# A fused RWKV5 and tanh-shrink kernel: u spread by TensorE, tile 0's first product by units, the last output in two parts, and a new written order

## The chip, the core and the metric

The kernel runs on one NeuronCore of a Trainium2 chip. The metric is device time in microseconds (us). Engines are named as the profile names them: PE is TensorE (PEld its weight loads), DVE is VectorE, ACT is ScalarE, POOL is GpSimd, SP is SyncE, which here only issues transfers; SPq and ACTq are the transfer-issuing instructions of SP and ACT.

## The reference, cut to what matters

```python
# attention: B, H, S, D = 4, 8, 768, 48; r, k, v float32; w, u are (H, D)
for t in range(S):
    cur = einsum('bhd,bhe->bhde', u[None] * k[:, :, t], v[:, :, t])
    y[:, :, t] = einsum('bhd,bhde->bhe', r[:, :, t], state + cur)
    state = w[None, :, :, None] * state + einsum('bhd,bhe->bhde', k[:, :, t], v[:, :, t])
x = y.transpose(0, 2, 1, 3).reshape(3072, 384)
# dense: w_in is (384, 2048), w_out is (2048, 384), both float64
h = x @ w_in
g = h - tanh(h)
out = g @ w_out          # (3072, 384) float32
```

## The kernel before, in words

**Units.** The sequence is cut into chunks of 64 steps. A unit `n` is one chunk of two of the four batches, 128 rows in all (function `unit`, with `ch, half = divmod(n, 2)`); there are 24. A unit loads r, k and v (`fetch`, L644, six transfers of 64 rows of 8 heads by 48 numbers), turns r and k by TensorE (`turn`, L656) into `x_ps`, scales them by powers of the decay into `rT` (DVE, L660) and `kT` (DVE L665, or an ACT copy, L692), forms the products of k and r within the chunk (`levels`, into `x_ps`, L606), masks them into `at` (DVE, L830) over a diagonal that ACT has written (`at`, L704) from `du`, the sum of r, k and u over a head (`rk`, L696; `rk` by `ub`, L824; `du`, L700), multiplies by v (`outputs`, into `yk_ps`), copies the result out (ACT: `xt` and `rest`, L765), and adds to the state (`state`, DVE, L792), which the next unit of the same two batches reads (`from_state`). Since `yk_ps` is one tile, a unit's `from_state` also waits until the unit before it has been copied out and added to its state. `ub` is u on all 128 partitions: before, one transfer at L568 writes it, reading u's 1536 bytes once for every partition. Units 0 and 1 differ: they have no state, and unit 0 takes its diagonal as a product with u (`own_k`, `own_levels`).

**Tiles of the dense part.** Two units make a token tile `j` of 256 rows. For each pair `f` of 128 columns of d_ff the function `hidden` makes h (`Dense.h`, L217, two halves of three products 128x256), g = h - tanh(h) in several ACT and DVE steps with a series for small h (L224 to L246), and the product with w_out (`Dense.o`, L254; later by a seven-product scheme, L307). The first tile of all is tile 0, f = 0 ("m == 0"); its h needs the `xt` of units 0 and 1 and the first piece of w_in.

**Weights.** w_in and w_out come as 64-bit floats in 16 pieces of 768 KB. A piece of w_in is two transfers on SP and two on POOL (`st`, L171); seven instructions turn it into float32: DVE L185, L186, ACT L187, L188, DVE L189, L190, L191 (`convert`).

**What sets the order.** All work is entered as tasks in a `Plan`; a table `ORDER`, two characters for each task, says in which order they are written (`written`). Each engine runs its own instructions in that order and waits where a tile is not ready. A number past the last task stands for a fill: a product of the identity that nobody reads, 512 or 256 columns wide (`fills`, L534), put where PE would have nothing to do. Transfers issued by SP and ACT take eight landing flags in turn (DMAHW0 to DMAHW7 in the listings below), so each waits until the one eight places before it has landed. 12 of the 24 units come before the seven-product part, one after another.

**The end.** The last tile (j = 11, f = 14) is done alone: `o` of the first 128 rows, then `o` of the second, each two products 128x384; DVE adds the sums of the rest (`empty`, L267 for the first half, L265 for the second) into `last`; after a branch that is not taken, four transfers (L1247) write `last` out, two on SP and two on ACT, 64 rows each.

Of the kernel before, what the change touches and what calls it, by code (L numbers as in the profile page):

```python
# [10 lines left out]
F32 = mybir.dt.float32  # L11
# [23 lines left out]
OWN = 1  # L35
SWAP = 2
# [9 lines left out]
    "00010J2i2j2k2f2g2h0H2m2l2nbWbW020K030I040605bWbX2q3435362o3231330A2s0F0B0C2r2ubWbX2x072v2y082w2t0T092z0L380M3U3C"  # L46
    "2+2p0N37393A3G2_3V3W0O3E0U3H3S3I3B3J3D3R3T3F0P3KbWbWbX3L0V3u3b300S3MbX3c3v3w0Q3N3a3f3s3O3g3P3r3t3e0R3Y3Q3hbX8D0w"
    "3d3i0W3k3X3Z3_3j0X4P430Y8E0d3l4O4Q0Z444L40458F4M4N3m0a463y0D0b3+3n0E0c423o41bY8P150e473x3z3p4p0f8H484Z4o4q0g4V4a"
    "0h494l8I4bbY4A4R0i4c4m4n4W3q4B4U0j4S4T8Q4v0l4C4X5I4Y4J4D4d8L4K5GbZ4e4I0k5J5K8R4F8G5F5H4f4H8J4G8KbZ4u8S134g4z8U8M"
    "8T4+4w4s4h0m8N4_4x4i8O4E5i4y4j5j5k500n525P4r4t8V4k5f8d8W515T0t0o5U8e536C0p5V5g5h8p8X5W5M0q6D6E5X540r8h5O0s555L5N"  # L50
    "5Q6A8q8Y56696B5R8Z5S5t5A6c578f5E5u5m8g5B5Y8i5v5lba5n595p8j5C8a585D6Z8b5Z8t0u6a6b8k8s5o5w8l6d6e5a8m8c6F5q5b6J8n14"
    "6N6G6H5r5c6O738o5s775d5x8w74755y6P8r8u915z6Q5e76786n8v6K6f8x5+6R6g6h6o6p6I5_926L7T8y7U7V609D7X6M67617W7Y6q6j656S"
    "7H636r0v687A668z6T956494936i98966U7IJx9762JyJz6k7J6V9EJ+6l6W8+J_K06m6X797B9G996s1D9H7h129F6Y9I9A9R907D7K6tKP9S9K"
    "7L7a9L6u9T7i9U7j0G7C0x9J7E6vKL9d7FKMKN0y8_7Z7b7d9e6w9MKOKQ9V726x9B7G6_1L9Y7k6z707M0zK16+719f9C7N9W9h9Z7c9X7e9iKs"
    "9a7O7lKu16K9K2K39N7PKAKvKw6y9O7g7fKrKt7QKZKa9r0+7RKR179g0_7m9Q9P9j9k9b187n10197o119s7p9l1T1U1E9c1F7q1A1G7vA19m7t"
    "9v1B7u1H7xA21C7w9u7y9t9n9yA41e1fKB1V9w1W1I1gKC1h9oLF1JA5LGLHAF9x1M9p1NA3AGA81O9z9qAR9+KDA6ASA7A9AJKb9_AIAAAUAMA0"
    "1PKc1QABAH1RAKAfAL1SATAg1iAVANAWAYAXAC1jADAZ1kArK6AEAaLIAhAsKWAi1xAOAkLJLKAjAPLl1lAmLmLnAnAQAuAvAtAyB3Aw1mAlB4Az"
    "AxLo1KLpLqAbB51XB6AoBFA+B71YB8BABG1Z1n1aBT1oBIBJBBAc2G2HBHL31p2FB9L4BUAdBMBKBCBf1bBWAeL5BVAp1cBYBXBNBgBLBaBbAqBi"
    "LTBh1dA_7S23241q2526B01rMABO1sKSKTB1BtBk1yBj1z1tBuB2Bm1+1uBD1_1vBZBE1wBlBvBcBPBy20KxBxBQBwKyKzBnBz2PB_2EC327B+28"
    "C4Bo29BRCH2A21C7BSCIC52BC6C0BdCK22CJCACLBe2XC82CM9MBCMCTCOC92ICN2DBp2J2QBq2RBr2SCUCPMf2TLzMgMhCBChCWCCCVBsCYCiCQ"  # L60
    "CXKdCbC1N3L+CZN4N52UC2CkCj2VCmCDCl2W2KCaCE2LCoCnCt2M2NCuCcD5CFCxCpCwCvCqD6CyCGC+CRD82OD7CzDK2Y2Z2aDL2bCSD92cDADC"
    "CdDBDDC_DZCfDM2dDNCe2eDaCgDECrD0DcDODFCsDbDRDGDdDPDgDoDQ85De86DpDfDS7rD1DrDhDq87EEDTD3DsDUDiEFDtDVDvD2EHDH81DuDW"
    "89ETEIDjEGELEJEUD4DkEK88EiDwEW8AEVDxDIEXEYDJDXEaDy7sDlEjEMENExEk8BElLUEmEy8CEZLVEnEbDYEoEqEzDmEpEOEcEPFNErE_DzE+"
    "FOF0EQF1D+F3DnFQ82FPD_F2EdFSE1EeFTE2FcF4EfFRE3E4E0FdE5EsE6EtE7ERE8FeEBFfE9FUFhESEuFVFgEDFrECFWF5FjEgF6FsEhFtFvEv"
    "FwFXFuFzFYFiEw7zFxEAG4FyF7FZFkG5Fl83F8FmG684G9FnG8F9F+G7FAGWGB7+FBGXFCFDFEFaFFGYGaFGFKGbGlGCGAFLGZF_FbGdFoGmGeGD"
# [1214 lines left out]
```

## Time and profile before

| what | us |
|---|---|
| median of 3 runs | 579.41 (578.5 to 583.4) |
| the profiled execution, whole | 582.91 |
| its span, from the first to the last instruction | 581.2 |
| PE busy in the span | 563.5 |
| DVE busy | 432.1 |
| ACT busy | 404.1 |

The profile has a page (busy time of each engine; the span in 40 slices; the chain that ended last), and answers by view: the timeline gives each instruction's start and length, with the idle time of its engine before it and what ended that; the view of waits adds these up; the view of windows gives each engine's busy time in a stretch, with the granted PE clock and the share of the core's 16 DMA engines (which can come out above 1). PE's busy time includes the fills, and a PE row `x6` is three products, since a float32 product is recorded in two passes.

### The profile page before, as it was taken

The page shows a single profiled execution, that of the slowest core. Times are in us where ns is not written, and L with a number is a line of the kernel's source. Part 1 is how long each engine was busy: PE and PEld are TensorE (multiplying, and loading weights), DVE is VectorE, ACT ScalarE, POOL GpSimd, SP SyncE. Part 2 cuts the span into 40 slices and gives each one's busy share as a digit, 9 for nine tenths or more (in the row PEclk, how much of TensorE's full clock was granted, in tenths as well). Part 3 has the DMA queues.
Part 4 walks back from the last instruction along what each step waited for, and adds up shares of the span by engine and source line. Part 5 has one row for each costly group of instructions (what it writes and reads, how often), then busy time and mean ns, then how long its engine had stood idle before and what let it go on. Part 6 is the DMA issues. An engine that isn't in the chain of part 4 may idle for free.

```text
span 581.2 us, 14164 instructions
## 1 busy us (share of the span) xinstructions
PE 563.5 (97%) x5487; PEld 481.5 (83%) x5487; DVE 432.1 (74%) x720; ACT 404.1 (70%) x926; POOL 202.5 (35%) x366
## 2 busy tenths in 40 slices
PE   7879999999999999999999999999999999999996
PEld 4557777777677789999899899999899898999994
DVE  5789977988999888776888897387685774565435
ACT  2689999998868666455784875766785668666560
POOL 5102211300000146353446355282454263554430
PEclk9899999999999999999999999999999999999998
DMA  8988657446640000032244352442123010010001
GB/s 130 162 204 137 125 100 189 103 76 167 114 120 15 1 1 12 17 55 41 40 74 86 62 94 39 72 86 39 25 50 60 16 34 7 3 29 2 14 16 32
DMA packets 138548, 38.48 MB, mean 66 GB/s; under 512 B 130760, under 2 KB 132904, under 8 KB 138472
## 3 DMA queue, kind: packets, MB, share of 16 engines
q1 hardware_dynamic: 130140, 29.71, 28.1%
q0 software_dynamic: 4992, 6.99, 5.3%
q10 hardware_dynamic: 3340, 0.79, 0.9%
q8 instruction: 45, 0.74, 0.5%
q14 instruction: 31, 0.25, 0.1%
HBM read 31.66 MB, written 4.72 MB: 63 GB/s over the span
## 4 chain that ended last, share of the span: by engine, by line
PE 79%; DMA 1%; ACT 1%; POOL 0%; DVE 0%; issue 0%; DVEq 0%; POOLq 0%
PE h L217 39%; PE p L307 28%; PE o L254 7%; PE yk_ps L606 5%; DMA xt<-rest 1%; PE p L254 0%; ACT xt L765 0%; POOL xt L786 0%; ACT rest L765 0%; ACT kT L692 0%; DVE rk L696 0%; DVE state L792 0%; DVE last L265 0%; PE x_ps L606 0%; DVEq L696 0%
## 5 line engine op out<-in xcount | busy, mean ns | idle before, releaser
L217 PE MATMUL h<-xt,w_in_sb 128*128 128x256 f32 x1152 | 269.0, 381 | 0.4 <-DMA xt<-rest 0.2
L217 PEld LDWEIGHTS h<-xt,w_in_sb 128*128 128x128 f32 x1152 | 214.8, 190 | 33.1 <-DVE w_in_sb L191 0.9
L290 POOL TENSOR_TENSOR sg<-g 128x256 f32<-128x256 f32 x69 | 55.9, 811 | 200.8 <-DVE g L246 147.0
L242 DVE TENSOR_TENSOR g<-h,th 128x512 f32<-128x512 f32 x96 | 65.8, 686 | 61.8 <-ACT tg L233 20.7
L229 ACT ACTIVATE s<-h 128x512 f32<-128x512 f32 x96 | 57.1, 595 | 54.5 <-PE h L217 40.0
L244 DVE TENSOR_TENSOR tg<-s,tg 128x512 f32<-128x512 f32 x96 | 71.7, 751 | 31.2 <-ACT s L224 27.7
L307 PE MATMUL p<-mixed,sg 128*128 128x192 f32 x426 | 93.0, 327 | 0.0
L246 DVE COPY_PREDICATED g<-small,tg 128x512 f32<-128x512 int32 x96 | 74.3, 783 | 12.6 <-ACT small L235 9.9
L231 ACT ACTIVATE th<-h 128x512 f32<-128x512 f32 x96 | 56.8, 593 | 35.0 <-PE h L217 34.7
L307 PEld LDWEIGHTS p<-mixed,sg 128*128 128x128 f32 x426 | 73.5, 190 | 1.4
L233 ACT ACTIVATE tg<-h 128x512 f32<-128x512 f32 x96 | 56.6, 592 | 22.9 <-DVE g L246 13.3
L307 PE MATMUL p<-w_out_sb,g 128*128 128x192 f32 x284 | 69.9, 328 | 0.0
L235 ACT ACTIVATE small<-s,smallb 128x512 f32<-128x512 f32 x96 | 68.5, 720 | 1.2
L254 PE MATMUL o<-w_out_sb,g 128*128 128x384 f32 x192 | 67.2, 489 | 0.1
L224 ACT ACTIVATE s<-s 128x512 f32<-128x512 f32 x96 | 60.1, 630 | 1.1
L786 POOL DMA_DIRECT2D xt<-rest x66 | 32.6, 498 | 68.9 <-ACT rest L765 68.4
L307 PEld LDWEIGHTS p<-w_out_sb,g 128*128 128x128 f32 x284 | 51.1, 190 | 2.7
L254 PEld LDWEIGHTS o<-w_out_sb,g 128*128 128x128 f32 x192 | 35.9, 190 | 19.4 <-issue 0.2
L704 ACT ACTIVATE at<-same,du 128x64 f32<-128x64 f32 x184 | 47.7, 340 | 5.0 <-DVE du L700 4.8
L292 POOL TENSOR_TENSOR sg<-sg,g 128x128 f32<-128x128 f32 x69 | 39.9, 581 | 3.6
L294 POOL TENSOR_TENSOR sg<-sg,g 128x128 f32<-128x128 f32 x69 | 38.1, 559 | 3.0
L307 PE MATMUL p<-w_out_sb,sg 128*128 128x192 f32 x142 | 34.9, 328 | 0.0
(127 smaller groups left out, 653.0 us busy)
## 6 DMA issues: line engine op xcount, KB each, us to landing
st<-in_moe_w_out_dram SPq DMA_DIRECT2D x8, 768.0 KB, 5.5
st<-in_moe_w_in_dram SPq DMA_DIRECT2D x16, 288.0 KB, 5.0
rt<-in_r_dram SPq DMA_DIRECT2D x46, 96.0 KB, 3.4
vt<-in_v_dram SPq DMA_DIRECT2D x46, 96.0 KB, 3.0
kt<-in_k_dram SPq DMA_DIRECT2D x44, 96.0 KB, 3.1
out_dram<-o POOLq DMA_DIRECT2D x44, 96.0 KB, 2.1
st<-in_moe_w_in_dram POOLq DMA_DIRECT2D x16, 96.0 KB, 5.8
parts<-in_k_dram SPq DMA_DIRECT2D x48, 32.0 KB, 2.1
```

Of the source, the lines that this page charges most:

```text
L217: self.nc.tensor.matmul(t.h2[:, z], self.w_in_sb[:, t.f // 2, kk, z * 128 : (z + 1) * 128], self.xts[t.j][:, kk].rearrange("p b t -> p (b ...
L224: A.activation(t.s, t.s, AF.Square, scale=G3)
L229: A.activation(out, t.h, AF.Arctan, scale=G2)
L231: A.activation(out, t.h, AF.Tanh)
L233: A.activation(out, t.h, AF.Tanh, scale=G1)
L235: A.activation(out, t.s, AF.Relu, bias=self.smallb, scale=-1.0)
L242: V.tensor_tensor(t.g, t.h, t.th, ALU.subtract)
L244: V.tensor_tensor(t.tg, t.s, t.tg, ALU.mult)
L246: V.copy_predicated(t.g, t.small.bitcast(I32), t.tg)
L254: self.nc.tensor.matmul(self.outs[i], t.g2[:, z, i * C : (i + 1) * C], self.w_out_sb[:, t.f + z, :], start=t.first and z == 0, stop=t.last ...
L290: add(t.s4[:, :2], g[:, 0::3], g[:, 1:2].to_broadcast([128, 2, C]), ALU.add)
L307: self.nc.tensor.matmul(ps[bank][:, half * n : (half + 1) * n], a, b, start=t.first and half == 0, stop=t.last, skip_group_check=True)
```

## The change

Four things are done together.

1. **u on all partitions by TensorE.** The transfer at L568 goes. u's rows already lie in the tile `rows` (with w's), loaded by the first transfers. Four small products of 8 rows by 96 columns, whose left side is a column of the identity repeated 128 times, put each row on all partitions, into a bank that unit 1 uses later; ACT copies it into `ub`.
2. **Tile 0's first h by units.** Its h, six products of 256 columns, becomes twelve of 128 columns: first the two halves for unit 0's rows, then the two for unit 1's. The fills that may stand there are entered anew.
3. **The last output in two parts.** `o` of the last 128 rows is made for columns 0 to 255 and then 256 to 383, and DVE adds each part as it is done. The last two transfers, 64 whole rows on each of SP and ACT before, become columns 0 to 255 of 128 rows on ACT and the other 128 columns on SP.
4. **A new table ORDER.** 15 fills (8 wide, 7 narrow) become 13 (8 wide, 5 narrow).

```diff
+LAST = 256
...
 ORDER = (
-    "00010J2i2j2k2f2g2h0H2m2l2nbWbW020K030I040605bWbX2q3435362o3231330A2s0F0B0C2r2ubWbX2x072v2y082w2t0T092z0L380M3U3C"
+    "00012j2k2l2g2h2i2m2n2o0I0Kbbbc020F030J040L2r36353706052p320G072s33342tbc080A0B0C2v2y092z0w2u382u393A0U2x0W2qbb2+0M"
...
-    def h(self, t, z):
+    def h(self, t, z, slot=None):
         d = self.d
+        if slot is not None:
+            if not hasattr(t, "h2"):
+                t.h2 = self.ps_d.tile([128, 2, d.NT], F32, name="h", tag="h")
+                t.h = t.h2.rearrange("p z t -> p (z t)")
+            for kk in range(d.NK):
+                self.nc.tensor.matmul(t.h2[:, z, slot * C : (slot + 1) * C], self.w_in_sb[:, t.f // 2, kk, z * 128 : (z + 1) * 128],
+                                      self.xts[t.j][:, kk, slot], start=kk == 0, stop=kk == d.NK - 1, skip_group_check=True)
+            return
...
-    def o(self, t, half):
+    def o(self, t, half, n=None):
...
-            self.nc.tensor.matmul(self.outs[i], t.g2[:, z, i * C : (i + 1) * C], self.w_out_sb[:, t.f + z, :],
-                                  start=t.first and z == 0, stop=t.last and z == 1)
+            cols = slice(0, self.d.DM) if n is None else n
+            self.nc.tensor.matmul(self.outs[i][:, cols], t.g2[:, z, i * C : (i + 1) * C], self.w_out_sb[:, t.f + z, cols],
+                                  start=t.first and z == 0, stop=t.last and z == 1, skip_group_check=n is not None)
...
+        if n is not None:
+            part = self.sums[at] if n.start == 0 else self.sums.pop(at)
+            a, b, op = (part, self.outs[i], ALU.subtract) if t.j in self.negative else (self.outs[i], part, ALU.add)
+            t.o = self.last[:, i]
+            self.nc.vector.tensor_tensor(t.o[:, n], a[:, n], b[:, n], op)
+            return
...
+    ub_ps = x_banks[1][:, 0, : H * D].rearrange("s (h d) -> s h d", h=H)
+
+    def spread_u():
+
+        for p in range(NP):
+            put_u = ident[: 2 * NP, NP + p : NP + p + 1].to_broadcast([2 * NP, 128])
+            T.matmul(ub_ps[:, 2 * p : 2 * p + 2], put_u, rows[:, :, :D], start=True, stop=True)
...
-        bonus = add("SP", .65, lambda: Q.dma_start(
-            out=ub.rearrange("p h d -> p (h d)"),
-            in_=bass.AP(tensor=u.tensor, offset=u.offset, ap=[[0, 128], [1, H * D]])), data=.7)
+        plan.at = "ub"
+        now = add("PE", .5, spread_u, landed, steps=16)
+        plan.at = None
+        bonus = add("ACT", .5, lambda: A.copy(ub, ub_ps), [now])
...
+            if m == 0:
+                now = add("PE", .66, lambda: dense.h(t, 0, 0), filled[j, "all"][:1] + [converted[piece]], due, steps=12)
+                plan.fills.append(([], now, fills(idle)))
+                now = add("PE", .66, lambda: dense.h(t, 1, 0), [now], due, steps=12)
+                now = add("PE", .66, lambda: dense.h(t, 0, 1), filled[j, "all"] + [now], due, steps=12)
+                plan.fills.append(([flagged], now, fills(tab)))
+                x.h = add("PE", .66, lambda: dense.h(t, 1, 1), [now], due + 1.3, steps=12)
...
+            whole = fs[1] == d.NF
+            if whole and j == d.NB - 1:
+                x.empty.append(add("DVE", .47, lambda: dense.empty(t, 0), [now], due + 3 * pace))
+                for n, cost, of in ((slice(0, LAST), .87, .38), (slice(LAST, d.DM), .43, .26)):
+                    now = add("PE", cost, lambda n=n: dense.o(t, 1, n), [now] + b1.emptied, due + 2 * pace + 1.3, steps=8)
+                    x.empty.append(add("DVE", of, lambda n=n: dense.empty(t, 1, n), [now, x.empty[-1]], due + 3 * pace))
+                x.o = now
+                return
...
-    for b in range(d.B):
-        queue = (nc.sync, nc.scalar)[b % 2]
-        queue.dma_start(out=out[(b + 1) * d.S - SHORT : (b + 1) * d.S, :],
-                        in_=shared["last"][b % 2 * SHORT : (b % 2 + 1) * SHORT, b // 2, :])
+    rows = out.rearrange("(b s) n -> b s n", b=d.B)[:, d.S - SHORT :]
+    for b in range(2):
+        (nc.sync, nc.scalar)[b].dma_start(out=rows[b], in_=last[b * SHORT : (b + 1) * SHORT, 0])
+    for queue, cols in ((nc.scalar, slice(0, LAST)), (nc.sync, slice(LAST, d.DM))):
+        queue.dma_start(out=rows[2:, :, cols], in_=last[:, 1, cols])
```

What the table does is seen in the instructions as each engine gets them. Numbers such as `first_k_123` or `rt_107` name the buffer: 122, 106, 116 are unit 0's k, r and v, 123, 107, 117 unit 1's, 108 and 118 unit 2's. Names of lines are those of each kernel; the changed one has them some 16 to 26 lines further down.

**Place 1: SP, the first transfers**, with what each waits for (a landing flag is named DMAHW). Before:

```order
L171 DMA st<-in_moe_w_in_dram 48x3x256 [waits DMAHW0_49]
L644 DMA vt_116<-in_v_dram 64x8x48 [waits DMAHW2_49]
L644 DMA first_k_123<-in_k_dram 64x8x48 [waits DMAHW4_49]
L644 DMA rt_107<-in_r_dram 64x8x48 [waits DMAHW5_49]
L568 DMA ub<-in_u_dram 128x384 [waits DMAHW6_49]
L644 DMA kt<-in_k_dram 64x8x48 [waits DMAHW7_49]
L644 DMA vt_117<-in_v_dram 64x8x48 [waits DMAHW0_49]
```

Now:

```order
L670 DMA vt_116<-in_v_dram 64x8x48
L172 DMA st<-in_moe_w_in_dram 48x3x256 [waits DMAHW0_49]
L172 DMA st<-in_moe_w_in_dram 48x3x256 [waits DMAHW1_49]
L670 DMA first_k_123<-in_k_dram 64x8x48 [waits DMAHW3_49]
L670 DMA rt_107<-in_r_dram 64x8x48 [waits DMAHW4_49]
L670 DMA vt_117<-in_v_dram 64x8x48 [waits DMAHW5_49]
L670 DMA kt<-in_k_dram 64x8x48 [waits DMAHW6_49]
```

ub is gone; the SP part of w_in's first piece, of which one transfer stood ahead of unit 0's k before, now follows unit 0's v; and unit 1's r waits for the landing of a transfer that was issued earlier.

**Place 2: ACT and DVE between unit 2's output and unit 3's start.** On ACT `at_133` is unit 3's diagonal, `xt`, `rest` are unit 2's output, `kT` is unit 3's, and `tg`, `s` belong to tile 0. Before:

```order
L229 ACT_TABLE_LOAD
L229 ACTIVATE s<-h 128x512
L704 ACTIVATE at_133<-same,du 128x64 x4
L765 COPY xt<-yk_ps 64x3x64 x4
L692 COPY kT<-x_ps_146 128x512
L765 COPY rest<-yk_ps 64x64 x4
L704 ACTIVATE at_133<-same,du 128x64 x4
L233 ACTIVATE tg<-h 128x512
```

Now:

```order
L242 ACTIVATE tg<-h 128x512
L730 ACTIVATE at_133<-same,du 128x64 x4
L791 COPY xt<-yk_ps 64x3x64 x4
L791 COPY rest<-yk_ps 64x64 x4
L718 COPY kT<-x_ps_146 128x512
L238 ACT_TABLE_LOAD
L238 ACTIVATE s<-h 128x512
L730 ACTIVATE at_133<-same,du 128x64 x4
```

The table load and `s` have moved from before unit 2's copies to behind them and behind unit 3's `kT`; `tg` has moved ahead. On DVE, at the same place and with what each waits for, before:

```order
L567 TENSOR_SCALAR flag<-h 1x1 [waits PE_49]
L191 TENSOR_TENSOR w_in_sb<-w_in_sb,power 128x768 [waits DVE_49]
L660 TENSOR_TENSOR rT<-x_ps_146,power 128x512 [waits Activation_49]
L185 TENSOR_SCALAR power<-st 128x768 [waits DMAHW6_49]
L792 TENSOR_TENSOR state_126<-yk_ps,state_126 128x8x48 [waits Activation_49]
L186 TENSOR_SCALAR w_out_sb<-st 128x768
```

Now:

```order
L686 TENSOR_TENSOR rT<-x_ps_146,power 128x512 [waits PE_49]
L192 TENSOR_TENSOR w_in_sb<-w_in_sb,power 128x768 [waits DVE_49]
L186 TENSOR_SCALAR power<-st 128x768 [waits DMAHW5_49]
L818 TENSOR_TENSOR state_126<-yk_ps,state_126 128x8x48 [waits Activation_49]
L187 TENSOR_SCALAR w_out_sb<-st 128x768
```

Unit 3's `rT` has moved ahead of the last step of w_in's second piece, and it waits for PE alone; before, it stood behind ACT's `kT`, which reads the same bank, and waited for ACT.

**Place 3: PE over the same stretch.** `at_132`, `vt_118` are unit 2's, `rt_106` unit 3's r; `state_127` is read by unit 3; L534 and L558 are fills. Before:

```order
L217 MATMUL h<-xt,w_in_sb 128x256 x3
L656 MATMUL x_ps_146<-ident,kw_113 128x128 x4
L606 MATMUL yk_ps<-at_132,vt_118 64x64 x16
L606 MATMUL yk_ps<-vt_118,kw_112 64x48 x16
L566 MATMUL h<-one,ok 1x1
L656 MATMUL x_ps_146<-ident,rt_106 128x128 x4
L534 MATMUL x_ps_150<-ident 128x512
L217 MATMUL h<-xt,w_in_sb 128x256 x3
L606 MATMUL yk_ps<-rT,state_127 64x64 x16
```

Now:

```order
L591 MATMUL h<-one,ok 1x1
L219 MATMUL h<-xt,w_in_sb 128x128 x6
L682 MATMUL x_ps_146<-ident,kw_113 128x128 x4
L632 MATMUL yk_ps<-at_132,vt_118 64x64 x16
L632 MATMUL yk_ps<-vt_118,kw_112 64x48 x16
L682 MATMUL x_ps_146<-ident,rt_106 128x128 x4
L558 MATMUL x_ps_150<-ident 128x512 x3
L632 MATMUL yk_ps<-rT,state_127 64x64 x16
```

The second half of tile 0's h has become the two parts for unit 1's rows, and tile 1's first h, which stood ahead of unit 3's start, now follows it; three wide fills stand there instead of one.

More of the change, by code (lines that the diff above doesn't have):

```diff
@@ L51 @@
[L51 to L65, printed above, removed]
@@ L548, in lay_out @@
                for e, at, x in (("SP", 0, w), ("ACT", NP, u))]
+        landed = now
         cols = add("PE", .25, lambda: T.transpose(cols_ps, rows.rearrange("p i d -> p (i d)"), ident[: 2 * NP, : 2 * NP]), now)
@@ L805, in unit @@
                 in_k = add("SP", 4.8, lambda: spread_out(k, 1), [b2.kT, *freed], data=.8)
-            x.turn = None if turned else add("PE", .46, lambda: turn(rt, r_ps), [x.r] + free, steps=8)
+            x.turn = None if turned else add("PE", .46, lambda: turn(rt, r_ps), [x.r] + free + [bonus] * (n == 1), steps=8)
             x.kw = add(*own_at, lambda: V_or_G.tensor_tensor(kw[:, :, :D], t.kt[:, :, :D], w_down, ALU.mult), [x.k, downs, b2.out])
@@ L920, in hidden @@
                 return
-            whole = fs[1] == d.NF
             for i in range(L):
```

81 lines of the change are left out of this document (48 added, 33 removed).

## The prediction

> **What bounds the kernel now.** I read the page's busy times and slices first, then the view of windows, then PE's waits.
>
> ```profile
> PE 563.5 (97%) x5487; PEld 481.5 (83%) x5487; DVE 432.1 (74%) x720; ACT 404.1 (70%) x926; POOL 202.5 (35%) x366
> ...
> PE   7879999999999999999999999999999999999996
> ```
>
> PE is busy for 97% of 581.2 us, and its digits are 9 from the fifth slice on: over the whole, TensorE bounds. The change takes no work from PE, so it can gain only where PE is not full: the first four slices (58 us) and the last. Windows show the first part:
>
> ```profile
> core 0: us, PE busy (x) PEld busy (x) DVE busy (x) ACT busy (x) POOL busy (x), PEclk, DMA share, GB/s
> 20.00:30.00 10.00, 7.72 (x139) 5.59 (x135) 6.94 (x13) 6.43 (x22) 1.78 (x4) 0.83 1.06 140
> 30.00:40.00 10.00, 8.22 (x184) 6.27 (x185) 7.92 (x15) 8.01 (x23) 0.00 (x0) 1.00 0.82 192
> 40.00:50.00 10.00, 8.59 (x219) 6.32 (x218) 9.51 (x16) 9.25 (x27) 3.43 (x7) 1.00 0.79 182
> 50.00:100.00 50.00, 49.12 (x932) 37.94 (x930) 42.47 (x76) 48.60 (x146) 9.17 (x19) 1.00 0.72 141
> ```
>
> PE loses 2.28, 1.78 and 1.41 us between 20 and 50, and some of its busy time there is fills; from 50 on it loses 0.88 us in 50. So the question is when PE gets to its first `o` of tile 0, from which on it is full:
>
> ```profile
> 50.21 2.75 PE L254 MATMUL o<-w_out_sb,g 128*128 128x384 f32 x8
> ```
>
> Whatever comes earlier at 50.21 comes off the end, as long as ACT, busy 48.60 of the 50 us behind it, keeps up. Before 50 PE is not the bound; what it waits for comes from DVE, and up to 30 us DVE waits for transfers.
>
> **Part A, the transfers (items 1 and 4, place 1).** DVE's waits that name a transfer, in its own in-order queue:
>
> ```profile
> 17.07 0.56 DVE L824 TENSOR_TENSOR rk<-rk,ub 128x384 f32<-128x384 f32 x1 [1.11 <-DMA ub<-in_u_dram]
> ...
> 27.56 0.56 DVE L185 TENSOR_SCALAR power<-st 128x768 uint32<-128x768 uint32 x1 [1.03 <-DMA st<-in_moe_w_in_dram]
> ...
> 29.82 0.56 DVE L696 TENSOR_TENSOR rk<-rt,kt 128x384 f32<-128x384 f32 x1 [0.76 <-DMA rt<-in_r_dram]
> ```
>
> 1.11 + 1.03 + 0.76 = 2.9 us. The first is u's copy itself, which goes. The other two are late because of a hole in the transfers:
>
> ```profile
> 8.00:12.00 4.00, 3.46 (x76) 2.35 (x75) 1.64 (x4) 2.08 (x7) 1.21 (x6) 1.00 1.21 165
> 12.00:16.00 4.00, 3.11 (x93) 2.58 (x92) 3.73 (x7) 2.20 (x4) 0.97 (x2) 1.00 0.56 123
> 16.00:22.00 6.00, 3.95 (x42) 2.12 (x42) 4.09 (x7) 3.32 (x13) 1.27 (x3) 0.96 1.16 191
> 22.00:30.00 8.00, 6.61 (x133) 4.89 (x131) 5.74 (x11) 5.25 (x16) 0.51 (x1) 0.82 1.04 125
> ...
> SPq L644 <- DMA vt<-in_v_dram: 2.6, 1, 2.6
> ...
> 10.81 0.59 SPq L644 DMA_DIRECT2D rt<-in_r_dram  x1
> ```
>
> The share (seventh value) is 1.21 and 1.16 on either side and 0.56 between: 4 x (1 - 0.56/1.18) = 2.1 us in which the queues ran dry, because SP stood 2.6 us at unit 1's r (until 10.81) for unit 0's v to land. Now that row waits for an earlier transfer, and SP can send unit 1's data and two of unit 2's without a stop. Without ub (128 times 1536 bytes, 196 KB, at 165 to 191 GB/s) another 1.0 to 1.2 us are free. Together 3.1 us, more than the 2.9 that DVE waits for, so the waits set the gain: at most 2.9, at least the 1.11 of ub alone. I take 2.0, the middle: the waits are in DVE's one queue and add up, but the work between them (5.74 of 8 us from 22 to 30) has releasers of its own on PE and ACT, which come into sight when the transfers are early. Against this stands w_in's first piece, which SP now sends behind unit 0's v; its conversion on DVE waits for no transfer before, and POOL's two parts of it stay where they are.
>
> The TensorE spread costs nothing on the path. Its four products stand where PE ran fills, and ACT's copy where ACT waited:
>
> ```profile
> 5.02 1.56 PE L534 MATMUL h<-ident 128*128 128x512 f32 x4
> 6.84 1.28 ACT L563 ACT_TABLE_LOAD   x1 [6.84 <-DVE power L554]
> 12.43 0.48 ACT L562 COPY w_down<-h 128x384 f32<-128x384 f32 x1 [0.74 <-PE h L529]
> ```
>
> A copy of the same shape takes 0.48 us and the table load 1.28; both fit into ACT's 6.84 us of waiting. If that cover were gone it would be 0.5 us. A DMA issue on ACT (unit 1's r) now stands in front of `kU` and waits for w_in's first part; behind it queue `kU` and `w_down`, which unit 0's output needs. That is part of why I stay below 2.9.
>
> **Part B, between unit 2's output and unit 3's start (place 2).** PE's longest wait in the region is for `state`, and this is what stands before it:
>
> ```profile
> 30.80 0.73 DVE L830 COPY_PREDICATED at<-before,x_ps 128x512 f32<-128x512 int32 x1 [0.41 <-PE x_ps L606]
> 32.25 1.28 ACT L229 ACT_TABLE_LOAD   x1 [1.86 <-PE h L217]
> 33.54 0.60 ACT L229 ACTIVATE s<-h 128x512 f32<-128x512 f32 x1
> 33.73 0.66 PE L656 MATMUL x_ps<-ident,rt 128*128 128x128 f32 x4
> 34.22 1.02 PE L534 MATMUL x_ps<-ident 128*128 128x512 f32 x2
> 36.29 0.59 ACT L692 COPY kT<-x_ps 128x512 f32<-128x512 f32 x1
> 36.77 0.86 ACT L765 COPY rest<-yk_ps 64x64 f32<-64x64 f32 x4
> 36.91 0.69 DVE L660 TENSOR_TENSOR rT<-x_ps,power 128x512 f32<-128x512 f32 x1 [1.63 <-ACT kT L692]
> 37.98 0.55 DVE L792 TENSOR_TENSOR state<-yk_ps,state 128x384 f32<-128x384 f32 x1
> 38.59 0.69 PE L606 MATMUL yk_ps<-rT,state 48*64 48x64 f32 x32 [1.69 <-DVE state L792]
> ...
> 31.53:37.98 6.45, 5.28 (x85) 3.56 (x84) 4.79 (x9) 5.60 (x17) 0.00 (x0) 1.00 0.86 196
> ```
>
> From the end of unit 2's mask (31.53) to `state` (37.98) DVE is busy 4.79 of 6.45 us; 1.63 of the rest is one wait of `rT` for ACT's `kT`, which came late because table load and `s` stood ahead of it. Now `rT` waits for PE's turn only. The same DVE work without the wait is 4.8 us: gain 1.6. It can't be more, since DVE is then full, and it is 0 if ACT's `rest`, which `state` also needs and which now comes before `kT`, is as late as before; its own chain gets shorter by 1.28 + 0.60 of load and `s` less 0.58 of `tg`, 1.3. I take 1.6, next to what DVE waits. The row at 34.22 is one wide fill, 1.02 us with its drain; three in a row are some 2.9. From the end of r's turn (34.39) to unit 3's start (38.59) PE has 4.2 us, and 4.2 - 1.6 = 2.6 when `state` is earlier, so the fills fill that wait and overhang it by 0.3, which is within what I leave open.
>
> **Part C, what is late next.** The 1.28 + 0.60 - 0.58 = 1.3 us of ACT's work have not gone but moved behind unit 3's `kT`, into a stretch where ACT is busy 9.25 of 10 us, with 0.75 free. So 1.3 - 0.75 = 0.55 is given back, at most 1.3, at least 0. I take 0.6. Tile 0's h by units costs PE a little (24 passes of 128 columns for 12 of 256), in a stretch where PE has waits; no term. The two narrow fills that go also stand there.
>
> **Part D, the end (item 3).**
>
> ```profile
> 572.65 2.74 PE L254 MATMUL p<-w_out_sb,g 128*128 128x384 f32 x8
> 573.61 0.35 DVE L335 TENSOR_TENSOR o<-o,p 128x192 f32<-128x192 f32 x1
> 574.14 0.56 DVE L267 TENSOR_TENSOR last<-p,o 128x384 f32<-128x384 f32 x1 [0.18 <-PE p L254]
> 574.72 1.79 SPq L1247 DMA_DIRECT2D out_dram<-last  x2
> 575.43 0.56 DVE L265 TENSOR_TENSOR last<-o,p 128x384 f32<-128x384 f32 x1 [0.73 <-PE p L254]
> ...
> DMA to landing us min/median/max: 3.9/4.0/4.1
> ```
>
> PE ends at 575.39, DVE's last add at 575.99, and the last two transfers, issued at 576.0, land 3.9 to 4.1 us later. The add of 128 columns instead of 384 takes about 0.28 (a third of the columns; the 192-column adds take 0.35), and the first part is added while PE makes the second. So the last issue is 0.28 earlier, and a third of the bytes is in it. Gain 0.3 for the add and 0.1 for the transfer, 0.4; at least 0.2, at most 0.8 if the shorter transfer lands earlier too.
>
> **Sum.** -2.0 - 1.6 + 0.6 - 0.4 = -3.4 us. The profiled execution took 582.91 as a whole (span 581.2), and would take 579.5. It is 3.5 above the median of the runs, 579.41, and the head and the end are alike in each run, so the forecast for the median is 576.0.
>
> **Rivals.** (1) *Only the end gains.* The head is held by DVE and ACT work, and transfers that come earlier only wait longer. For it: DVE is busy 9.51 of 10 between 40 and 50. Against it: the 1.63 and 2.9 of named waits lie in DVE's own queue. Time: the end's 0.4, 579.0.
>
> (2) *Everything goes at once.* A whole (2.9), B whole (1.6), nothing given back, 0.8 at the end, and the waits of PE that name no releaser vanish:
>
> ```profile
> PE x_ps L606 <- issue: 1.3, 1, 1.3
> ```
>
> 2.9 + 1.6 + 0.8 + 1.3 = 6.6, 572.8. Against it: those waits have no cause that the change touches.
>
> (3) *ACT becomes the bound, slower.* Place: 50 to 100, where ACT is busy 48.60 and idle 1.4 us. The new table orders ACT's rows anew; if ACT is left idle there as it is between 30 and 50 (1.99 + 0.75 in 20 us, 6.9 in 50), PE waits for the g of the tiles, 6.9 - 1.4 = 5.5 us, and -3.4 becomes +2.1: 581.5. It decides from 4.8 us of idle ACT on. Against it: PE's order there has the first h of tile 5 with one more `o` pair ahead of it than before, so the worst known place gets easier.
>
> (4) *The fills hold PE up.* The change then does not do what its table says: it is written for one timing of the transfers, and where data comes earlier the fills stand in PE's queue. Price: the overhang of 0.3 at the three wide fills, and at most two more places with a wide fill, 1.02 each: 2.3 at most, 1.2 in the middle, so 577.2. For it: DVE's waits in part A depend on transfers, whose times vary. Against it: two fills fewer.
>
> (5) *The clock falls once more.* PE's thin stretch from 18 on ends in a slow clock:
>
> ```profile
> 22.00:24.00 2.00, 2.00 (x52) 1.65 (x50) 1.97 (x5) 0.00 (x0) 0.44 (x1) 0.50 1.21 156
> ...
> 21.57 1.11 PE L656 MATMUL x_ps<-ident,kw 128*128 128x128 f32 x4 [0.90 <-DVE kw L807]
> ```
>
> Granted 0.50 for 2 us, and a turn takes 1.11 instead of 0.66. The stretch 20 to 30 has 0.83, which is 1.7 us of clock lost in 10. Another such stretch, with PE on the path, costs 1.7 us: 577.7. For it: two fills fewer. Against it: DVE paces that part. The Trainium skill, "TensorE: Matmul & The Clock Gate", section "What's actually happening", says the clock drops to half after about 3.4 us of idling and needs as long of work to come back. The trace agrees with the half (0.50); no run here shows the 3.4.
>
> **Numbers.** Forecast 0.50, (1) 0.19, (2) 0.11, (3) 0.07, (4) 0.08, (5) 0.05. The time is 576.0. The range reaches from (2), 572.8, up past (1) to 580.4, which cuts off part of (3) and of the spread of the runs (578.5 to 583.4). A measurement here tells about 1% (5.8 us) from no change. Faster by more than that (below 573.6) needs (2), 0.11, or the forecast with its terms at their lower bounds, 0.09: 0.20. Slower (above 585.2) needs (3) with nothing gained ahead of it, 579.41 + 5.5 - 0.4 = 584.5, and more: 0.05. Same: 0.75.
>
> **What would show it.** Right: no wait of `rk` for ub; a DMA share near 1 from 12 to 16; DVE's waits on st and rt below 0.5 each; unit 3's `state` at about 34 to 35 instead of 37.98, with no wait of `rT` for `kT`; the first `o` at about 47.2; the last add 0.28 us behind PE. Wrong: the first `o` later than 49.5; or that `o` early but PE idle by more than 3 us between 50 and 150; or the two last transfers landing later than 4 us after their issue.

## The result, and the profile after

The changed kernel takes 584.61 us (median of 20 runs, 582.43 to 588.09), the kernel before 580.32 (577.17 to 583.62, 20 runs on the same chip). The ratio is 1.0065 [1.0047, 1.0083], so the change costs 3.8 us [2.7, 4.8]. The forecast was 576.0, 3.4 us below, and its range ended at 580.4: it was wrong in sign. The profiled execution took 584.97 as a whole, with a span of 583.2.

The page first, then the windows, in the columns of the rows shown for the kernel before:

```profile
PE 565.2 (97%) x5507; PEld 483.9 (83%) x5507; DVE 434.0 (74%) x721; ACT 406.0 (70%) x927; POOL 207.1 (35%) x366
...
PE   6989999999999999999999999999999999999994
```

```profile
12.00:16.00 4.00, 2.99 (x70) 2.11 (x68) 1.51 (x3) 1.64 (x5) 1.35 (x3) 1.00 1.17 187
20.00:30.00 10.00, 9.90 (x219) 7.75 (x218) 9.93 (x18) 8.37 (x29) 0.51 (x1) 1.00 1.11 207
30.00:40.00 10.00, 9.29 (x221) 6.66 (x220) 8.78 (x16) 9.87 (x27) 0.00 (x0) 1.00 0.77 173
40.00:50.00 10.00, 8.81 (x157) 6.18 (x156) 9.68 (x18) 9.74 (x31) 3.94 (x8) 1.00 0.71 141
50.00:100.00 50.00, 49.92 (x969) 38.00 (x971) 44.30 (x78) 49.00 (x147) 9.62 (x19) 1.00 0.71 141
100.00:150.00 50.00, 48.75 (x288) 36.44 (x278) 44.80 (x69) 44.28 (x87) 6.50 (x13) 1.00 0.54 110
...
577.00:578.00 1.00, 0.00 (x0) 0.00 (x0) 0.00 (x0) 0.00 (x0) 0.00 (x0) 0.60 0.14 41
579.00:580.00 1.00, 0.00 (x0) 0.00 (x0) 0.00 (x0) 0.00 (x0) 0.00 (x0) 0.50 0.15 48
```

The head looks as forecast: the hole in the transfers from 12 to 16 is filled (share 1.17 for 0.56), and PE is busy 9.90, 9.29 and 8.81 us of the three tens up to 50, for 7.72, 8.22 and 8.59. Two things are new: PE is idle for 1.25 us between 100 and 150, and behind the work the transfers run at a share of 0.14, long after PE and DVE have stopped. The timeline of the changed kernel:

```profile
9.86 1.12 PE L682 MATMUL x_ps<-ident,rt 128*128 128x128 f32 x4 [2.31 <-DMA rt<-in_r_dram]
...
34.63 0.69 PE L632 MATMUL yk_ps<-rT,state 48*64 48x64 f32 x32
...
47.34 2.75 PE L264 MATMUL o<-w_out_sb,g 128*128 128x384 f32 x8
...
574.96 0.62 DVE L274 TENSOR_TENSOR last<-o,p 128x256 f32<-128x256 f32 x2 [0.75 <-PE p L264]
575.41 1.08 ACTq L1288 DMA_DIRECT2D out_dram<-last  x1
575.60 0.63 SPq L1288 DMA_DIRECT2D out_dram<-last  x1
```

The first `o` stands at 47.34, 2.87 us earlier than 50.21. The last add ends at 575.58, only 0.41 earlier than 575.99. And from there to the end of the span it is 7.6 us (583.2 - 575.58), where it was 5.2 (581.2 - 575.99). So 2.5 us of the head are lost between 47 and 575, and 2.4 more behind the last add. While the last transfers move, the share is 0.14 to 0.15; before, from 576 to 577, it was 0.69:

```profile
576.00:577.00 1.00, 0.00 (x0) 0.00 (x0) 0.00 (x0) 0.00 (x0) 0.00 (x0) 1.00 0.69 193
```

PE's waits from 50 to 583 say where it stood in the middle, now:

```profile
PE h L226 <- DVE g L251: 1.5, 3, 0.7
PE h L226 <- DMA xt<-rest: 1.2, 1, 1.2
```

and before:

```profile
PE x_ps L656 <- issue: 0.8, 1, 0.8
PE yk_ps L606 <- DVE state L792: 0.3, 1, 0.3
PE h L217 <- DMA xt<-rest: 0.2, 1, 0.2
```

The timeline ends the new ones at 113.60 (1.25 us, the transfer), 411.74 (0.60), 475.75 (0.17) and 559.39 (0.74). They add up to 2.8 us where the old ones add up to 1.3, so they account for 1.5 of the 2.5 that are lost in the middle. The other 1.0 stands in no wait of PE that the profile shows, and its cause stays open.

### The profile page after: what moved, and what is told of

The parts are those of the page before. It is cut to its first block, busy times and chain, and to the rows that moved or that the text cites. A ratio compares the mean times of both kernels' runs of the same rounds, so it can differ in the third digit from the quotient of the medians.

```text
span 583.2 us, 14198 instructions
## 1 busy us (share of the span) xinstructions
PE 565.2 (97%) x5507; PEld 483.9 (83%) x5507; DVE 434.0 (74%) x721; ACT 406.0 (70%) x927; POOL 207.1 (35%) x366
## 4 chain that ended last, share of the span: by engine, by line
PE 79%; ACT 6%; DVE 6%; issue 3%; DMA 3%; POOL 1%; ACTq 0%; SPq 0%; DVEq 0%; POOLq 0%
PE h L226 37%; PE p L323 23%; PE o L264 9%; PE yk_ps L632 6%; ACT at L730 1%; PE x_ps L682 1%; DVE g L255 1%; DMA rt<-in_r_dram 1%; DVE g L251 1%; DMA xt<-rest 1%; PE h L558 1%; PE x_ps L632 1%; DVE tg L253 1%; DMA st<-in_moe_w_in_dram 1%; ACT tg L242 1%
## 5 line engine op out<-in xcount | busy, mean ns | idle before, releaser
L226 PE MATMUL h<-xt,w_in_sb 128*128 128x256 f32 x1140 | 263.7, 381 | 2.8 <-DVE g L251 1.5
L253 DVE TENSOR_TENSOR tg<-s,tg 128x512 f32<-128x512 f32 x96 | 70.5, 736 | 24.8 <-ACT s L233 17.9
L308 POOL TENSOR_TENSOR sg<-sg,g 128x128 f32<-128x128 f32 x69 | 43.3, 632 | 3.5
L310 POOL TENSOR_TENSOR sg<-sg,g 128x128 f32<-128x128 f32 x69 | 38.8, 568 | 3.3
L361 POOL DMA_DIRECT2D out_dram<-o x44 | 24.1, 549 | 37.7 <-DVE o L351 21.8
```

The source lines that it names most:

```text
L226: self.nc.tensor.matmul(t.h2[:, z], self.w_in_sb[:, t.f // 2, kk, z * 128 : (z + 1) * 128], self.xts[t.j][:, kk].rearrange("p b t -> p (b ...
L253: V.tensor_tensor(t.tg, t.s, t.tg, ALU.mult)
```

## The experiments

Twelve kernels ran, and each was compared with the kernel before on the same chip. "Stretch" is the time from the start of the first `o` to the end of DVE's last add; "end" is from there to the end of the span.

### The end: shapes and parts

**e1_rows**, the changed kernel with other shapes at the end:

```diff
-    for queue, cols in ((nc.scalar, slice(0, LAST)), (nc.sync, slice(LAST, d.DM))):
-        queue.dma_start(out=rows[2:, :, cols], in_=last[:, 1, cols])
+    for cols in (slice(0, LAST), slice(LAST, d.DM)):
+        for b, queue in ((0, nc.scalar), (1, nc.sync)):
+            queue.dma_start(out=rows[2 + b][:, cols], in_=last[b * SHORT : (b + 1) * SHORT, 1, cols])
```

> The changed kernel, with each of its two last transfers (2x64x256 and 2x64x128) cut into two of 64 rows (64x256 twice, 64x128 twice). Theory A, that a transfer whose outermost dimension is 2 is carried by about two DMA engines: the stretch from DVE's last add to the end falls from 7.6 us to about 5.2, the DMA share there goes from 0.11-0.15 to 0.5 or more, and the ratio to the kernel before goes from 1.0065 to about 1.002. Rival B, that the short rows (1024 and 512 bytes) are slow by themselves: the stretch stays at 7 us or more and the ratio at 1.006. In both the middle keeps its loss.

Measured: ratio 1.0002 [0.9973, 1.0032], end 5.3 us (span 581.1). The windows of this kernel's end:

```profile
576.00:577.00 1.00, 0.00 (x0) 0.00 (x0) 0.00 (x0) 0.00 (x0) 0.00 (x0) 1.00 0.70 191
577.00:578.00 1.00, 0.00 (x0) 0.00 (x0) 0.00 (x0) 0.00 (x0) 0.00 (x0) 0.71 0.56 142
```

The same 1024- and 512-byte rows move at 191 GB/s when the outermost dimension is 64. Rival B, the short rows, falls.

**e2_whole_end**, the changed kernel with the last output whole (four matmuls of 384 columns, one add, the old transfers of 64x384):

> The changed kernel, with the last output whole again: four matmuls of 128x384, one add, and two transfers 64x384 behind it, as before the change. Theory A: the end's 2.4 us come back and the ratio is about 1.002, the same as with the shapes alone mended, since the two parts by themselves are worth at most 0.4 us. Theory C, that the parts are worth what the forecast gave them once the transfers are mended: this kernel is 0.4 to 0.8 us slower than the one with the shapes mended. Rival, that the written order loses everything in the middle: the ratio stays at 1.005 or more.

Measured: 0.9985 [0.9957, 1.0012], end 4.65 us. The end's cost is gone. This is faster than the 1.002 that theory A gave, and the interval just excludes that. Theory C, that this kernel is 0.4 to 0.8 us slower than e1_rows, falls: its median is 1.25 us shorter (580.47 for 581.72). So does the rival of 1.005 or more. Whether the parts themselves cost something isn't settled by this pair, since the two intervals overlap; e11_before_parts below has them alone.

**e3_before_pair**, the kernel before, with one transfer in the place of the last two (the minus lines stand for b = 2 and 3):

```diff
-        queue.dma_start(out=out[(b + 1) * d.S - SHORT : (b + 1) * d.S, :],
-                        in_=shared["last"][b % 2 * SHORT : (b % 2 + 1) * SHORT, b // 2, :])
+    nc.sync.dma_start(out=rows[2:], in_=last[:, 1])
```

> The kernel before, with its last two transfers (64x384 each, on two queues) replaced by one 2x64x384. Rows stay at 1536 bytes. Theory A (outermost 2 means about two engines): 196 KB at some 40 GB/s instead of 200 makes the end 3 to 4 us longer, ratio 1.005 to 1.007. Rival B (short rows): no change, ratio 1.000 +/- 0.001.

Measured: 1.0035 [1.0008, 1.0061], +2.0 us where 3 to 4 were expected; end 7.5 us for the 5.2 of before. Its windows:

```profile
576.00:577.00 1.00, 0.00 (x0) 0.00 (x0) 0.00 (x0) 0.00 (x0) 0.00 (x0) 0.50 0.12 38
577.00:578.00 1.00, 0.00 (x0) 0.00 (x0) 0.00 (x0) 0.00 (x0) 0.00 (x0) 0.50 0.14 52
```

Rows of 1536 bytes and only the outermost dimension changed: the share is again 0.12 to 0.14, about 2 of 16 engines (0.14 x 16 = 2.2). Theory A stands, at a smaller price than it gave. The Trainium skill has this rule, in "DMA: Bandwidth & Descriptors", section "Why a DMA increments its semaphore by 16 and not by 1": a transfer runs on the largest number of engines up to 16 that divides the slowest dimension on both sides. For 2 on the side of `out` and 128 partitions on the side of `last` that is two engines, and the trace agrees.

**e12_before_parts_pairs** and **e11_before_parts** put the change's end alone on the kernel before, as written and with 64-row transfers:

```diff
+    x.o:   dense.o(t, 1, slice(0, LAST)); dense.o(t, 1, slice(LAST, d.DM))
+    empty: dense.empty(t, 1, slice(0, LAST)); dense.empty(t, 1, slice(LAST, d.DM))
```

> The kernel before with the change's end alone: the last output in columns 0 to 255 and 256 to 383, both adds behind both products as in the changed kernel, and the two transfers 2x64x256 and 2x64x128. Theory A: from PE's end to the span's end 8.1 to 8.4 us instead of 5.2 to 5.9, so 2.3 to 2.8 us slower, ratio 1.004 to 1.005. If the end were a gain as forecast (0.4 us): 0.999 to 1.000, and the middle alone would have to explain the changed kernel.

> As e12_before_parts_pairs, but each of the two transfers cut into two of 64 rows, on both queues. Forecast's part D, rightly shaped: DVE's last add ends 0.35 us behind PE instead of 0.60, and the time is 0.2 to 0.8 us shorter than before, ratio 0.9985 to 0.9995. Theory K, that the parts bring nothing even then, since both adds wait for the second product and two more issues follow: the last add ends 0.62 to 0.68 behind PE, PE's end to the span's end takes 5.8 to 6.2 us, and the ratio is 1.000 to 1.001.

Measured: as written 1.0061 [1.0034, 1.0087], +3.5 us [2.0, 5.1]; with 64-row transfers 1.0007 [0.9985, 1.0028]. The adds of the second, and then of the first:

```profile
572.62 0.62 DVE L266 TENSOR_TENSOR last<-o,p 128x256 f32<-128x256 f32 x2 [0.75 <-PE p L256]
```

```profile
572.30 0.62 DVE L266 TENSOR_TENSOR last<-o,p 128x256 f32<-128x256 f32 x2 [0.75 <-PE p L256]
```

Both adds start behind PE's last product (PE ends at 572.58 and 572.26) and take 0.62 us together; the one whole add takes 0.56. Nothing of the first add runs under the second product: both adds are written behind both products, here and in the changed kernel's table (its last five tasks are the first half's add, the two products, the two adds). No run has the first add written between the two products. The end is 5.4 us with 64 rows and 7.6 with pairs. Theory A's 1.004 to 1.005 lies in the interval of the kernel with pairs. Theory K stands: rightly shaped, the parts change nothing that these runs can tell.

### The middle: head and body of the written order

**e5_old_body** has the change's head, the old end, and from tile 0's first `o` on the old order. **e6_new_body** is the kernel before, its own head and end, with the new order behind that `o`. Of the program only the table changes:

```diff
 e5:  ORDER = new[: first o of tile 0] + [what is left, as the old table orders it]
 e6:  ORDER = old[: first o of tile 0] + [what is left, as the new table orders it]
```

> The changed kernel with its last output whole again (as in e2_whole_end), and with the new written order kept only up to tile 0's first output matmul; everything behind it stands in the old kernel's order. Theory F, that the new order of the body makes the four waits of PE at 111, 410, 475 and 558 us: they go, the stretch from the first o to DVE's last add falls from 528.1 us to 525 (+/- 0.5), and the time falls by 2 to 3 us against e2_whole_end, to a ratio of 0.993 to 0.996 to the kernel before. Rival G, that the waits come from the head being earlier, whatever the body's order: the waits stay within 10 us of these places or come elsewhere, the stretch stays at 527.5 to 528.5 and the ratio at 0.998 to 1.000.

> The kernel before, its own head and its own end, with everything behind tile 0's first output matmul in the new kernel's order. Theory F: the four waits come up here too, near 111, 410, 475 and 558 us, the stretch from the first o to DVE's last add goes from 525.0-525.8 to about 528, and the ratio is 1.004 to 1.006. Rival G: no such waits, the stretch stays below 526, ratio 1.000 +/- 0.001.

Measured: e5_old_body 0.9958 [0.9935, 0.9981], which is -2.4 us [-3.8, -1.1]; e6_new_body 1.0045 [1.0019, 1.0071], +2.6 us [1.1, 4.1]. First `o` and last add, then PE's waits, of e5_old_body:

```profile
47.30 2.75 PE L264 MATMUL o<-w_out_sb,g 128*128 128x384 f32 x8
...
572.33 0.55 DVE L281 TENSOR_TENSOR last<-o,p 128x384 f32<-128x384 f32 x1 [0.73 <-PE p L264]
```

```profile
PE yk_ps L632 <- DVE state L818: 1.0, 2, 0.6
PE h L226 <- DMA xt<-rest: 0.3, 1, 0.3
```

and of e6_new_body:

```profile
48.27 2.75 PE L254 MATMUL o<-w_out_sb,g 128*128 128x384 f32 x8
...
576.18 0.56 DVE L265 TENSOR_TENSOR last<-o,p 128x384 f32<-128x384 f32 x1 [0.73 <-PE p L254]
```

```profile
PE h L217 <- DVE g L242: 1.8, 3, 0.9
PE h L217 <- DMA xt<-rest: 1.0, 1, 1.0
```

The stretch is 525.58 with the old body behind the new head, and 528.47 with the new body behind the old head. The four waits go with the body, at 114.28, 412.98, 476.99 and 560.63 in e6_new_body; the 0.3 for `xt` in e5_old_body, at 114.35, is a wait that the kernel before has too (0.2). Theory F stands and rival G falls, though e5_old_body's ratio is only 0.0027 below e2_whole_end's, 1.6 us where 2 to 3 were expected. Over all profiles but one, below, the stretch has two values: 525.0 to 525.9 in the nine kernels with the old body, 528.1 to 528.5 in the four with the new one, whatever the head and the end were.

**e9_two_places** goes into one step more. It is e2_whole_end with three instructions moved:

```diff
 DVE:  g of tile j=8, f=2     ahead of kT, kT, rT, rT of unit 20
 ACT:  th of tile j=11, f=10  ahead of s, its square and small of tile j=11, f=12
 DVE:  g of tile j=11, f=10   ahead of m of tile j=11, f=12
```

> As e2_whole_end (the new order throughout, the last output whole), with three instructions moved and nothing else: near 410 us DVE's g of the tile that PE's h waits for stands ahead of the four instructions that turn a unit's k and r, and near 557 us ACT's th and DVE's g of the tile that h waits for stand ahead of the next tile's s, its square and small. Theory H, that the waits of h are the order of DVE and ACT at these two places: the gaps of 0.59 and 0.74 us go, those at about 112.8 (1.07) and 475 (0.17) stay, and the stretch from the first o to DVE's last add falls from 528.1 to 526.8 (+/- 0.3); the time falls by 0.6 to 1.3 us, to a ratio of 0.996 to 0.998. Rival J, that PE asks for h too early there, so that g can't be ready whatever stands ahead of it: each gap shrinks by less than 0.3 us and the stretch stays at 527.7 or more.

Measured: 0.9947 [0.9925, 0.9969]. DVE and PE near 410 us in e2_whole_end:

```profile
406.88 0.73 DVE L255 COPY_PREDICATED g<-small,tg 128x512 f32<-128x512 int32 x1
407.50 0.69 DVE L706 STREAM_TRANSPOSE kT<-parts 128x512 f32<-128x512 f32 x1
408.23 0.79 DVE L707 TENSOR_TENSOR kT<-kT,inverse 128x512 f32<-128x512 f32 x1
408.94 0.70 DVE L706 STREAM_TRANSPOSE rT<-parts 128x512 f32<-128x512 f32 x1
409.68 0.74 DVE L707 TENSOR_TENSOR rT<-rT,power 128x512 f32<-128x512 f32 x1
410.34 0.68 DVE L251 TENSOR_TENSOR g<-h,th 128x512 f32<-128x512 f32 x1
...
411.07 2.21 PE L226 MATMUL h<-xt,w_in_sb 128*128 128x256 f32 x9 [0.59 <-DVE g L251]
```

and in e9_two_places, with its first `o` and last add:

```profile
47.29 2.75 PE L264 MATMUL o<-w_out_sb,g 128*128 128x384 f32 x8
...
408.12 0.68 DVE L251 TENSOR_TENSOR g<-h,th 128x512 f32<-128x512 f32 x1
408.72 0.70 DVE L706 STREAM_TRANSPOSE kT<-parts 128x512 f32<-128x512 f32 x1
...
410.96 1.24 PE L226 MATMUL h<-xt,w_in_sb 128*128 128x256 f32 x5
...
573.04 0.55 DVE L281 TENSOR_TENSOR last<-o,p 128x384 f32<-128x384 f32 x1 [0.73 <-PE p L264]
```

Four instructions of a unit, 2.84 us from 407.50 on, stood in DVE's queue ahead of the `g` that reads the `h` of two tiles ago, and PE's next `h` waits for that reader. With `g` ahead PE doesn't wait, and the wait near 558 is gone too. The stretch is 526.30 for 528.12; 1.33 of this 1.82 are the two waits, and where the other 0.5 comes from stays open. The stretch and the ratio fell further than theory H gave (526.8 +/- 0.3, 0.996 to 0.998; the interval reaches into the latter). What is left is 0.98 near 113 and 0.16 at 475, together 1.1 us and so no more than the old body's 1.3, and yet the stretch is longer than the old body's 525.0 to 525.9: here too something is lost that no wait shows. Theory H stands for the two waits.

### The head: u's copy, and tile 0's h

**e7_old_body_u_dma** is e5_old_body with u's copy by DMA, **e8_old_body_h_whole** is e5_old_body with tile 0's `h` whole, at the place of the second unit's parts:

```diff
 e7: - PE spread_u, ACT copy          + SP dma_start(ub <- u, 128 x 384)
 e8: - h(t, 0, 0), h(t, 1, 0), h(t, 0, 1), h(t, 1, 1)     + h(t, 0), h(t, 1)
```

> As e5_old_body, but u comes to all partitions by the DMA of the old kernel; the two TensorE and ScalarE steps are left out. The forecast's step A and rival 1 disagree on it. If the small transfers are what delays the head: 1 to 2.9 us slower than e5_old_body, and the first o 1 to 3 us later than 47. If u's DMA is hidden in this head: within 0.5 us of e5_old_body.

> As e5_old_body, but tile 0's first products are made whole (six matmuls of 256 columns behind both units) at the place where the second unit's parts stand. If the split by units buys the head nothing now that it is bound by transfers: within 0.5 us of e5_old_body. If PE lacked work while the second unit was made: the first o is 0.6 to 1.3 us later, and the time 0.6 to 1.3 us longer.

Measured: e7_old_body_u_dma 581.08 us beside 579.04 of e5_old_body (0.9986 [0.9961, 1.0011] and 0.9958 [0.9935, 0.9981]); its first `o`:

```profile
50.04 2.75 PE L264 MATMUL o<-w_out_sb,g 128*128 128x384 f32 x8
```

2.7 us later than 47.30, and 2.0 us in the median: u's DMA is worth as much as the whole of part A, and more than the 1.11 that part A had for u's own wait, though the two intervals overlap. Part of it is a row that part A had named. ACT issues unit 1's r at 11.52 for 9.92, and `kU`, behind it in ACT's queue, starts at 12.72 for 11.11; PE waits 3.00 us for `kU`, where it waits 1.88 in e5_old_body. The 2.7 itself is one profile, of one of the three longest of that kernel's twelve executions (582.84).

e8_old_body_h_whole took 579.65 (0.9975 [0.9950, 1.0001]), 0.6 more than e5_old_body, which these runs can't tell from nothing. But its profile, of its longest execution (582.62), has the first `o` 3.0 us later than e5_old_body's, where at most 1.3 was expected:

```profile
28.00:32.00 4.00, 4.00 (x32) 3.22 (x24) 3.97 (x7) 2.10 (x4) 0.00 (x0) 0.62 0.81 106
...
50.28 2.75 PE L264 MATMUL o<-w_out_sb,g 128*128 128x384 f32 x8
```

PE stands idle for 1.66 us up to 27.11, where e5_old_body makes the first parts of h (25.13); then the granted clock falls (0.62 from 28 to 32), and the whole h takes 4.54 us from 28.35 on. Of the twelve executions five took 581.71 to 582.62 at a mean granted clock of 0.989 to 0.992, and seven 577.50 to 579.73 at 0.994 and more. So the split by units may well be worth some 3 us in some executions and nothing in others; with twelve of each kernel that isn't shown. And u's DMA is not the only thing that can put the first `o` at 50.

**e4_before_u** is the kernel before with nothing but u's spread and copy, at the DMA's place in the table; **e10_early_u** has the spread right behind the turn of w and u.

```diff
-        bonus = add("SP", .65, lambda: Q.dma_start(out=ub..., in_=u on 128 partitions), data=.7)
+        bonus = add("SP", .65, spread_u, data=.7)       # e10: the spread behind cols, A.copy(ub, ub_ps) ahead of "saved"
```

> The kernel before, with u's copies by TensorE and ScalarE in the place of the small DMA, in the old order. Theory D, that the head's gain of 2.9 us is the transfers' and does not reach the end because the body eats it: unit 0's wait for u goes, the first o of tile 0 comes 0.5 to 2 us earlier than 50.2, and the ratio is 0.998 to 1.000. Rival E, that what comes earlier at the first o comes off the end in full when the old body order is kept: the ratio falls by as much as the first o moves, 0.997 to 0.999 for 0.5 to 2 us.

> The kernel before, old order and old end, with u's spread on TensorE right behind the turn of w and u, in the place of one wide fill, and ScalarE's copy ahead of the small copy of w. Beside e4_before_u it takes away ACT's wait of 1.76 us for the spread, which stood ahead of kU. If that wait counts: kU at 8.6-9.5 instead of 10.57 us, the first o 0.3 to 1 us earlier than 46.97, ratio 0.993 to 0.995. If transfers set the pace of the head: the first o stays at 47 (+/- 0.3) and the ratio is that of e4_before_u, 0.995 (+/- 0.001). In either case the stretch from the first o to DVE's last add is 525.0 to 525.8, the old order's.

Measured: e4_before_u 578.93 us, 0.9953 [0.9920, 0.9987], first `o` at 46.97, stretch 524.99. Theory D, that the body eats the gain, is wrong for the old body; rival E holds, with more than the 0.997 to 0.999 that it gave (the interval reaches into that), though the one profile of before can't say how far the first `o` moved. e10_early_u 579.51, 0.9981 [0.9953, 1.0008]: `kU` comes at 10.27 for 10.57 and the first `o` at 47.55, outside both forecasts, and the ratio is not better than e4_before_u's. Without its 1.76 us of waiting for the spread, ACT stands 1.29 us for DVE's `kT` instead, so taking that wait away brought nothing that shows.

## Why the prediction was wrong, step by step

Three experiments carry one part each: the new head -2.4 us (e5_old_body), the new body +2.6 (e6_new_body), the new end +3.5 (e12_before_parts_pairs). That is +3.7, and the changed kernel measured +3.8. So the parts make the whole; that they do to 0.1 is luck, as each is known to some 1.5 us.

| step of the forecast | forecast | measured |
|---|---|---|
| A + B + C, the head | -3.0 | -2.4 [-3.8, -1.1] |
| D, the end | -0.4 (-0.2 to -0.8) | +3.5 [2.0, 5.1]; 2.4 in the profiles |
| the body, "whatever comes earlier at 50.21 comes off the end" | 0 | +2.6 [1.1, 4.1] |

**The head was right in sum.** No wait for ub, st or rt is left on DVE, the share is 1.17 from 12 to 16, unit 3's `state` is at 34.02 (PE reads it at 34.63) and the first `o` at 47.34, where 34 to 35 and 47.2 were forecast. In this execution unit 0's r landed late: PE waits 2.31 us for it, and DVE 3.35 behind PE. In e5_old_body, with the same head, PE waits 0.37 us for r and 1.88 for `kU`, and by tile 0's h, at 25.30 and 25.13, the two executions are 0.17 us apart.

The parts of the head are not shown to be right. u's spread alone, in the old order, brought 2.7 us [0.8, 4.7] (e4_before_u), and all the rest of the new head, with u's DMA kept, 0.8 [-0.6, 2.3] (e7_old_body_u_dma). By the forecast the rest was worth more: B less C is 1.0, and part A had up to 1.8 for transfers other than u's. No run tried B or C alone. "No term" for tile 0's h by units has no run behind it either, as e8_old_body_h_whole shows. So that the sum came out near is in part luck. Its terms were read from one profile of before, and that was a late one: in e3_before_pair, with the same head,

```profile
47.26 2.75 PE L254 MATMUL o<-w_out_sb,g 128*128 128x384 f32 x8
```

The five profiles with before's head and its DMA have the first `o` at 47.26, 47.72, 47.80, 48.27 and 50.21. So "the head and the end are alike in each run" was wrong. The -2.4 is what runs of the kernel give; a size taken from one trace of it could have been anything between 0 and 2.9.

**Part D failed in both of its terms.** "the first part is added while PE makes the second", and in the list of changes "DVE adds each part as it is done": the table has both adds behind both products, and the last one ends 0.66 us behind PE, where it was 0.60 before and 0.28 was forecast. "a third of the bytes is in it": the transfer has the outermost dimension 2 and ran on about two engines. The bounds 0.2 to 0.8 left out a loss, because I priced the transfer by its bytes and not by its shape. The sign that I had named for it, landing later than 4 us after the issue, was there: the two were issued at 575.41 and 575.60, the share is still 0.15 from 579 to 580, and the span ends at 583.2.

**The body failed by what I didn't look at.** I followed the new table up to the first tiles and took the rest as unchanged. It orders all five engines anew to the end. The nearest rival, ACT as the bound between 50 and 100, had the place wrong (ACT is busy 49.00 of 50 there and PE loses 0.08) and the mechanism too: where PE waits more than before, it is for single rows of DVE and ACT far behind, at 410 and 558 (shown by moving them), and for one row at 113. Of that last one only the place is known: PE stood 1.25 us for the transfer of `xt`, and in e1_rows and e9_two_places at the same place for `g`. These waits are 1.5 of the 2.5 us; the rest of the body's loss goes with its order, but the step that causes it stays open. The sign that I had named, PE idle by more than 3 us between 50 and 150, looked at the wrong stretch: it was 1.3 there. The rivals of the fills and the clock did not come up in this profile: the three wide fills end at 34.62, 0.05 us behind `state`, and the granted clock is 1.00 from 20 to 150.

The experiments also show versions that beat both kernels: u's spread alone (e4_before_u, 0.9953), the new head with the old body and end (e5_old_body, 0.9958), and the new order with two places mended and the old end (e9_two_places, 0.9947). Their intervals overlap, and none is shown to be the best.

## What to carry to other kernels

When an order is written anew, look for each wait of the bounding engine along the whole of it: here the new body took about as much as the head had gained, and more than half of that stands in four waits of PE, up to 500 us behind the place that the change was about. Look at the shape of a transfer that nothing stands behind, not only at its bytes: put a long dimension outermost. And take sizes of a start-up phase from several executions, or from an experiment with that part alone; one profile had it 1.9 to 3.0 us later than four others.

## What was not expected of the hardware

Two transfers of the same shape (64x384, the last two) brought the end to 3.7 us behind the last add in one profile (e9_two_places) and to between 4.65 and 5.5 in the eight others with this end. Why it landed sooner there stays open.

PE's granted clock fell to half at different places in executions of the same head. In e5_old_body it did from about 12 on, after a thin stretch:

```profile
8.00:12.00 4.00, 1.72 (x48) 1.41 (x52) 1.52 (x3) 1.41 (x5) 0.96 (x5) 0.92 1.24 160
12.00:16.00 4.00, 4.00 (x72) 2.38 (x71) 2.90 (x6) 0.76 (x3) 1.58 (x5) 0.50 1.30 183
```

For the changed kernel, with the same head, the column says 1.00 from 12 to 16, but its rows don't bear that out up to about 14. The turn of r takes 1.12 us at 9.86, where it takes 0.66 in e5_old_body at 6.58, and two rows of products of the same shape take 1.13 and then 0.69:

```profile
12.61 1.13 PE L632 MATMUL x_ps<-rT,kT 48*64 48x64 f32 x32
...
14.76 0.69 PE L632 MATMUL x_ps<-rT,kU 48*64 48x64 f32 x32 [1.01 <-DVE at L856]
```

So PE ran slowly there too, earlier in the head, and a 1.00 in the column has to be checked against the lengths of the rows. The first `o` came at 47.30 and 47.34 in the two, but as both had a slow stretch, this doesn't say that one costs nothing: in e8_old_body_h_whole the half clock fell on tile 0's h, and the first `o` came at 50.28.
